# Two grouped-query attention blocks on one core: remainder scores in groups of three steps, remainder of P by DMA in some steps, output tiles kept in the accumulator

## The chip, the core and the metric

The kernel runs on one core of a Trainium2 chip. The metric is device time in microseconds (us) of one execution. Before the change the median of three runs is 721.26 us (721.23 to 722.15). The engines are named as in the profile: PE is TensorE (matrix multiply), PEld its weight loads, DVE is VectorE, ACT is ScalarE, POOL is GpSimd, and SP is SyncE, which here only issues DMAs.

## What is computed

There are two independent problems, A and B, of the same shape: 16 batches, 80 query rows each, model width 576, 32 query heads, 16 key/value heads, 512 cached keys, head width 128, all in bf16.

```python
q = (x @ wq).reshape(B, Sq, Hq, Dh).transpose(0, 2, 1, 3)
k = jnp.repeat(k_cache, rep, axis=1)          # rep = 2
v = jnp.repeat(v_cache, rep, axis=1)
scores = jnp.einsum("bhqd,bhkd->bhqk", q, k) * (Dh ** -0.5)
p = _softmax(scores, axis=-1)
o = jnp.einsum("bhqk,bhkd->bhqd", p, v)
out = o.transpose(0, 2, 1, 3).reshape(B, Sq, Hq * Dh) @ wo
# result: concatenate([out_A, out_B], axis=-1)
```

## The kernel before

**Steps.** The work is cut into 128 steps U, 64 for each problem. A step is one batch and four key/value heads, so 4 x 160 = 640 rows of scores (two query heads of 80 rows share one key/value head) against 512 keys. The 640 rows are taken as five tiles of 128: tiles 1 to 4 hold the first 128 of the 160 rows of each key/value head, and tile 0, the *remainder*, holds the last 32 rows of all four heads. 512 keys of one tile fill one PSUM bank; there are eight banks.

**What a step does on each engine.**
- SP loads K for two steps in one DMA transpose (1 MB, L626) and V for one step in a plain DMA (512 KB, L630).
- PE makes the scores. Tiles 1 to 4 are one full 128x128 matmul of 512 columns each (`qk`, L673). The remainder is four matmuls of 32 output rows side by side in the array (`qkr`, L660). The remainder scores of a *group* of steps are issued together; the sizes of the groups come from `GRP` (the first ones) and `GR` (all others), and a group takes one PSUM bank for each of its steps.
- DVE takes the row maximum (L682), ACT the exponential with its row sum (L686), DVE the reciprocal (L692), POOL the scaling (L695, `nrm`). The result is P in bf16, in `p_sb`: `NPA` slots for tiles 1 to 4 and `NPR` slots for remainders.
- PE transposes P (`tr`, L727): 40 small transposes in a step, 8 for each tile, each of a 64-row half. They go in pairs, one for each half of the array's rows. Each half has one PSUM bank for tiles 1 to 4 (`vtp`) and one for the remainder (`vtq`). DVE or ACT copies the first into `pT` (`ptev`, L738 or L740) and the second (`prev`, L745 or L747).
- PE multiplies by V (`pv`, L770, 4 x 4 matmuls of 160 columns), and DVE or ACT copies the result into `oT` (`oev`, L784).

**Beside the steps.** The projection of Q (`qp`, L537, four matmuls of 320 columns for one head and half a batch group; `qt`, L550, two 64-row matmuls that add the last 64 of the 576 input columns) is spread over the steps as 128 sessions. A session before step `US0` has its `qt` for itself (`pre`), a later one has it at the head of the transposes of a step, and shares the two banks `vtq` with the remainder's transposes. DVE or ACT then evicts Q (`qev`, L563 or L564). The output projection (`op`, L816, 2 x 8 matmuls of 288 columns for an output tile) runs twice for each problem over eight head pairs; the first pass lands in `acc` (L828), the second is added to it on DVE into one of two buffers `osb` (`oeb`, L845) and stored by SP (`st`, L851). x is loaded first, into the memory of `acc`, in pieces that `XLD` places.

**The order.** Nothing is decided at run time. Each operation is added to a list with the stream it belongs to, and the string `ORDER` says, letter by letter, which stream is next; an apostrophe takes the second engine of an operation that DVE or ACT may do, a digit gives the PSUM bank. That sets the order on every engine and the buffers' waits: an engine stops at an instruction until the semaphores for what it reads, and for the buffer it writes, have come. The constants `LA`, `GRP`, `TS0` and the like set keys within a stream.

Of the kernel before, what the change touches and what calls it, by code (L numbers as in the profile page):

```python
# [11 lines left out]
GRP = (1, 1, 2)  # L12
GR = 2
LA = 11.5
# [3 lines left out]
NPR = 4  # L18
NPT = 2
# [11 lines left out]
US0 = 2  # L31
# [16 lines left out]
XLD = ((-100.0, -60.0), (-5.0, -4.9))  # L48
# [11 lines left out]
LETTERS = "abcdefghijklmnopqrstuvwxyzABCDEFGHIJKLMNO"  # L60
ORDER = """
nEKni7KHHHHHHNj3Ej4IMk5j6MNIj7j3Mk4ILd6Id5IIdd2AaBd1dd5BAd6dd2'Bd1dd6BMd0AdAd7'BAd5Ldd4'A'Bd6dd5'ABKMd7add3'AB
d4e0doe1'Be2'Ad5ole7of6ld3ole0pe1dlod4omd2Ke7A'BhdCloe6vhf5Cald3oud0lBupf12luAdme7puo'BOmg0456Cpu'Ae1y'wOe3'xl
vj0oj4d5'zuCMj7loe6ud0moue1dMlk2Md4Llok7e2c3'AFBcle6hod5a'sLldog0137'BAe2'yCd5CCvw'zoj3e0lue7Mj4o'xve3lc6Mcuc1
locuof24ld0tu'spc7lucpg16muCtme3uzd2'youe7e6'wd4'xho'AFlg15oalBc3Cz'xe0u'wcle7Bc5uoc'yf46v'ACsle1oud2'tpd3ulc5
# [12 lines left out]
15z'w'ye2pb3'x'Bhomc7hCAculae0e1od4ubplComuc6e0qd2luog35slCuf17x'yBc'wu'zpe0d3'tomc5cCpc6u'Ae2le1scvod4'tvog05
lhuhle6zb2a'yCoume1we0vod5'x'Bc7Aulcoc4cld3t'se6e1log47ole0bCCo'wulzud6'x'yBe1u'Ae7Coc4ld3uo'qe5hvclag02sulof1
4u'wxlAc7cp'yb6p't'ze0e7moe2c5cBlbCouod3lvCc1slue0qcd5omuhhf27tlug46pe0y'wb1'zC'xou'Be6mFbvolue2qc4'Ae5olcac3s  # L80
d1CCpcud4'toulg06vb3'wzluA'xue2me6Bboyld4oe1Fc7od5lhqg02lf36'wz'Ae1xcCoc4u'sce2Blhud7od5'tp'ye1Ke4lob0mCoue2bl
puolvg13lc4z'ycc2q'se1acmoe0e4b3xlCCou'td6Bulwd2ovg15AluCf07w'zCve4'ype5b'AuomFoue1lKc6xd0uKo'qe4lhd3uolcuBc5c
'se2ltg16aob5p'w'zClxuc4ce6u'se2obmCB'Aud4olve0Cc7lod3u'ycug26ltrf17'ywChxve0'zpc5h'AcuDoe2'Be6'sc4oumck3ohuc5
lctd1'sLle0c4d5loe2coalg36C'tud0w'zyue4'xd6'Bolg35AlCpuc2c'yze1vc4'w'xoe3'Ab5umolBe0coc7'te6e1lscCe4oule2baoul
oe0ld3Coud6'sClrug17oluCf45z'yvc2p'wc'xd7uA'tmc1Bucpe2lc3vFoce6mDud4thloe0hg35soe2'zb1o'x'yCwe5luBbColue6lrud3
oDd4luhe0'Ag12holaCf57luyc6z'wvc'x'Ae0pc1'sue2'Bcome6c3pd4lCcCou'td5moug01lsue7z'wc3'xuclBd2ov'Ae1'yd5olg46Ctu
lhf07zhv'ye3pc1'wud4'Aomce2pc6lcod0'shC'xe3tu'Bc1aocle6ub5Cslvome1uc3ocg27u'te3'yzbloe2lrb7ole1e6loe5e3bDolaCC
xlb2uo'Buod6'wluCAd1lruc4g05uf37uy'zc'xwvd5Bpe0bhpmDAc1csd3C'thrumCg46JouDlf12xuwBc7'yczue0e4sc3cpb7'thoGc3ole
6bolCAe0luce5sb4urvoDe7d3ovle6boalome0d5Crlpg14lb7wx'ACov'zc3e6ucoe4'tbu'yomuBc3crhluc5CDe1d7luoclsd2hCvlg36DJ
u'tf04y'w'Aue1'ze5oe7ue3b6Caolupbluomd5xr'Bc1olcd6Cpluc2cvg07tsue2zme1b3Gw'xC'yoJue7oKd4luc0Blcoe2c6'Ascle1oe5  # L90
d0'tolg67oCe2z'xbulov'w'Be1re7'Aud0lCod3ulyKg45uClohuf26Jw'yxKCe1'zupc4hc'ABuc5mae0pcvlc3ocud2ts'sle7d3ome5Cg1
4ovlc6ulxcwod0u'Be7A'yd3o'te1lzg26lCouf45'w'zxd7Aulpe6hc0'yDcoc1'Bacsme2Cc3puclc0ok4umctd6vC'sLe1lug35'toue4'z
e0ob2lo'ye5we1lCbxuBloue6e4'Aoc3lacd7olc5ocld0sC'te1rulg36ovf25'yzue4lpe3b6wmxpc1'Acoh'Bd2mhCCc7svDe0lochud5o'
te1lug47oluCe3xblyuo'zue0e1'wBd4luaod5'Aole7g23rlof06'wz'yc1'xCcp'Auc3le2Bcuc4C'sod5mupe1clue0Coc7mcvhsd2Dot't
ve4lDg67uhlohd3ux'yhze1e0'Bd6o'wlc7oe2lcAc4c'sCoe5ulhg17tulof04v'zCxb2p'wulyd7u'BAmc5pe1cc3msce0ohe6'td5oalg34
olCe1ub'zo'yvxle0wd3CuB'Arc4lucoe2c7uod5le1'scolg06tlCf24zu'yDe7pe1uhb6xamwvCobuplud2Cmrc7uoe0'Ae6c'BuCoc3lcuo
d4lsug15lCtvf07'x'yve6p'wb3'zuBhobuDAlFe1c4moce2e6lod5d0olc1rclDg23t'shpe1'ye6Cwb4umAxuze2'BboCoc7lucc3lsvd5rc
uoe0Dd4thlg67oaf12w'zCCub3'xp'Avyme7e5uobloule1rc6ulcod3Be0lc7Cocud4'tslCg15vhDe7u'zxb6ao'wu'ACyle0e5bpomd3r'B
c7oe1lcoc4'se2d6lCovcg07u'tluf45w'xy'zd1uF'Bpe0luhd7Ac6moucpg23'slc4ze6cob0yle3FbmoaC'tCe2xule6oe5b4uolure3'wb
louolvd2CBe0'Aud6qloug57f14z'x'Bc3y'wc'Ae7d6'sDold3hCplue2c5Ccomug07hplvc1t'xucC'zwe2c5'yuod7'Bcu'se0lthe3uc1o  # L100
ac'Ac5'socme2d6tloe1b4Cloue0lvg35oluby'zxlwe1Ce2uo'Bf35'Aoue0ld6qvFld7phc4ocmc2se1lcpg34htae0y'zb2'xC'w'BuAc3m
# [165 lines left out]
def bass_concat_heads__gqa_block_cached__gqa_block_cached__near_ridge_kernel(  # L267
# [27 lines left out]
    with ExitStack() as es:  # L295
# [32 lines left out]
        def R(res, ver):  # L328
            return (res, ver)
# [281 lines left out]
        for U in range(NSU):  # L611
# [103 lines left out]
            def em_tr(e, psls=tuple(psls), vtq=vtq, vtp=vtp, td=td):  # L715
# [214 lines left out]
```

## Time and profile before

| | value |
|---|---|
| median of three runs | 721.26 us |
| the profiled execution | 722.56 us |
| its span, first to last instruction | 720.6 us |
| granted clock of TensorE | 1.000 |
| PE busy | 715.3 us, 99% of the span |
| DVE and ACT busy | 641.3 and 639.8 us, 89% each |
| POOL busy | 432.6 us, 60% |
| DMA moved | 160.73 MB |

The profile was taken in one execution. Busy time of PE is made of modelled ends: a matmul's record lasts longer than the time until the next one may start, because matmuls are pipelined, so what a matmul costs in a row of others is read from the starts. An engine's idle time is given with the instruction that released it. DMA issues are those of SP; "to landing" counts from the issue to the last byte.

### The profile page before, as it was taken

What the parts mean: (1) busy time and instruction counts of PE and PEld (TensorE: products, weight loads), DVE (VectorE), ACT (ScalarE), POOL (GpSimd) and SP (SyncE); (2) the same over time, 40 slices, a digit from 0 to 9 for tenths busy, and PEclk for the clock granted to TensorE, in tenths of its full rate; (3) what the DMA queues carried; (4) which work ended last, traced back from release to release, by engine and by line L of the source; (5) the groups of instructions that cost most, each with busy time, mean ns of one, the idle gap of its engine ahead of it and who ended that gap; (6) DMA issues with size and microseconds to landing.
All of it is one profiled execution on the core that took longest, in us unless ns stands there. A gap on an engine that the chain in (4) does not pass through costs nothing.

```text
span 720.6 us, 26290 instructions
## 1 busy us (share of the span) xinstructions
PE 715.3 (99%) x10820; PEld 513.1 (71%) x10820; DVE 641.3 (89%) x1459; ACT 639.8 (89%) x1844; POOL 432.6 (60%) x650
## 2 busy tenths in 40 slices
PE   9999999999999999999999999999999999999998
PEld 5567767777677777777777777777777777777777
DVE  3999998899888998899998899979999889998995
ACT  1999999799989998789997899989999889998993
POOL 0477755566556675665675567646676656755773
PEclk9999999999999999999999999999999999999999
DMA  9999999899999999999999998999999898988860
GB/s 248 268 269 259 265 255 241 206 189 259 225 241 209 217 254 240 226 254 205 268 207 219 248 245 212 247 236 204 181 262 224 193 241 198 220 194 200 178 199 18
DMA packets 374167, 160.73 MB, mean 223 GB/s; under 512 B 278560, under 2 KB 370976, under 8 KB 374048
## 3 DMA queue, kind: packets, MB, share of 16 engines
q1 hardware_dynamic: 374048, 159.05, 95.6%
q8 instruction: 86, 1.41, 0.8%
q14 instruction: 33, 0.27, 0.1%
HBM read 87.65 MB, written 2.95 MB: 126 GB/s over the span
## 4 chain that ended last, share of the span: by engine, by line
PE 98%; ACT 1%; issue 0%; DVE 0%
PE ps L816 22%; PE ps L770 20%; PE ps L537 19%; PE ps L673 16%; PE ps L727 11%; PE ps L660 5%; PE ps L550 4%; ACT p_sb L686 1%; PE ps L348 0%; PE ps L396 0%; ACT qT L563 0%; PE ps L414 0%; PE ps L451 0%; DVE osb L845 0%; DVE wo_sb L341 0%
## 5 line engine op out<-in xcount | busy, mean ns | idle before, releaser
L695 POOL TENSOR_SCALAR p_sb<-p_sb,rinv 128x512 bf16<-128x512 bf16 x640 | 430.8, 694 | 272.7 <-DVE rinv L692 272.2
L686 ACT ACTIVATE p_sb<-ps,negmax 128x512 bf16<-128x512 f32 x640 | 444.0, 711 | 29.8 <-DVE negmax L682 25.5
L682 DVE TENSOR_REDUCE negmax<-ps 128x1 f32<-128x512 f32 x640 | 419.2, 681 | 27.5 <-PE ps L673 22.2
L770 PE MATMUL ps<-pT,v_sb 128*128 128x160 bf16 x2048 | 191.1, 233 | 0.1
L770 PEld LDWEIGHTS ps<-pT,v_sb 128*128 128x128 bf16 x2048 | 154.0, 98 | 39.5 <-ACT pT L745 3.3
L816 PE MATMUL ps<-wo_sb,oT 128*128 128x288 bf16 x1280 | 181.6, 286 | 0.0
L673 PE MATMUL ps<-kT,qT 128*128 128x512 bf16 x512 | 176.4, 381 | 0.0
L537 PE MATMUL ps<-xT,wq_sb 128*128 128x320 bf16 x1024 | 176.0, 299 | 0.0
L816 PEld LDWEIGHTS ps<-wo_sb,oT 128*128 128x128 bf16 x1280 | 122.1, 98 | 43.2 <-ACT p_sb L686 1.7
L686 ACT ACTIVATION_READ_ACCUMULATOR p_sb<-ps,negmax 128x1 f32 x640 | 144.0, 225 | 0.0
L537 PEld LDWEIGHTS ps<-xT,wq_sb 128*128 128x128 bf16 x1024 | 94.5, 98 | 42.4 <-ACT p_sb L686 2.2
L727 PEld LDWEIGHTS ps<-ident,p_sb 64*128 64x128 bf16 x5120 | 91.4, 95 | 8.8 <-issue 1.1
L727 PE MATMUL ps<-ident,p_sb 64*128 64x64 bf16 x5120 | 96.1, 190 | 1.2 <-ACT qT L563 0.7
L738 ACT COPY pT<-ps 128x512 f32<-128x512 f32 x150 | 88.4, 603 | 9.4 <-PE ps L727 9.0
L740 DVE COPY pT<-ps 128x1024 bf16<-128x1024 bf16 x106 | 72.0, 684 | 13.2 <-PE ps L727 11.7
L563 ACT ACTIVATE qT<-ps 128x320 bf16<-128x320 f32 x131 | 59.5, 462 | 16.2 <-PE ps L550 15.4
L784 DVE CAST oT<-ps 128x320 bf16<-128x320 f32 x129 | 61.5, 482 | 6.5 <-PE ps L770 6.0
L564 DVE TENSOR_SCALAR qT<-ps 128x320 bf16<-128x320 f32 x125 | 59.5, 482 | 8.1 <-PE ps L550 6.6
L673 PEld LDWEIGHTS ps<-kT,qT 128*128 128x128 bf16 x512 | 48.4, 97 | 25.7 <-issue 3.3
L784 ACT CAST oT<-ps 128x320 bf16<-128x320 f32 x127 | 56.4, 448 | 10.2 <-PE ps L770 9.9
L745 ACT COPY pT<-ps 128x128 f32<-128x128 f32 x132 | 36.1, 288 | 7.0 <-PE ps L727 6.8
L692 DVE RECIPROCAL rinv<-rowsum 128x3 f32<-128x3 f32 (+1 forms) x256 | 39.5, 161 | 2.3 <-ACT p_sb L686 2.2
(31 smaller groups left out, 194.7 us busy)
## 6 DMA issues: line engine op xcount, KB each, us to landing
v_sb<-in_A_v_cache_dram SPq DMA_DIRECT2D x64, 512.0 KB, 5.4
v_sb<-in_B_v_cache_dram SPq DMA_DIRECT2D x64, 512.0 KB, 4.9
wo_sb<-in_A_wo_dram SPq DMA_DIRECT2D x8, 576.0 KB, 5.6
wo_sb<-in_B_wo_dram SPq DMA_DIRECT2D x8, 576.0 KB, 5.6
wq_sb<-in_B_wq_dram SPq DMA_DIRECT2D x4, 1024.0 KB, 6.6
out_dram<-osb SPq DMA_DIRECT2D x40, 72.0 KB, 3.4
wq_sb<-in_A_wq_dram SPq DMA_DIRECT2D x8, 256.0 KB, 4.5
wq_sb<-in_A_wq_dram SPq DMA_DIRECT2D x2, 1024.0 KB, 7.3
```

The source lines that it names most:

```text
L537: last = e.matmul(ps[:, vbq[h].phys, QO:QO + 320], lhsT=wq_sb[:, wsl, ck, hi * 128:(hi + 1) * 128], rhs=xT[:, half, ck, n0:n0 + 320], star ...
L563: return e.activation(dst, src, AF.Identity, scale=SCALE)
L673: return e.matmul(ps[:, vb.phys, :], lhsT=qT[:, qsl, bl, gl * 160:gl * 160 + 128], rhs=k_of(U, gl), start=True, stop=True)
L682: return e.tensor_reduce(negmax[:, si:si + 1], ps[:, vb.phys, :], axis=AX.X, op=AluOpType.max, negate=True)
L686: return e.activation(p_sb[:, psl, :], ps[:, vb.phys, :], AF.Exp, bias=negmax[:, si:si + 1], scale=1.0, accum_out=rowsum[:, ss, k:k + 1])
L695: return e.tensor_scalar(p_sb[:, psl, :], p_sb[:, psl, :], rinv[:, ss, k:k + 1], 1.0, op0=AluOpType.mult, op1=AluOpType.mult)
L727: last = e.matmul(dst, lhsT=p_sb[64 * h:64 * h + 64, psls[k_], j * 128:(j + 1) * 128], rhs=ident[64 * h:64 * h + 64, 64 * h:64 * h + 64], ...
L738: return e.copy(pT[:, pts, :, :].bitcast(F32)[:, :, 32 * h:32 * h + 32], ps[:, vtp[h].phys, :].rearrange("p (n c) -> p n c", n=16))
L740: return e.tensor_copy(pT[:, pts, :, 64 * h:64 * h + 64], psb[:, vtp[h].phys, :].rearrange("p (n c) -> p n c", n=16))
L770: last = e.matmul(ps[:, vo.phys, off:off + 160], lhsT=v_sb[:, vs, gl, j * 128:(j + 1) * 128], rhs=pT[:, pts, 4 * gl + j, :], start=(j == 0 ...
L784: return (e.copy if en == "act" else e.tensor_copy)(dst, src)
L816: last = e.matmul(ps[:, vb.phys, 0:DC], lhsT=oT[:, sp_ * (HH // 2) + i, rb * 128:(rb + 1) * 128], rhs=wo_sb[:, 2 * c3 + sp_, i, :], start= ...
```

## The change

- `GRP` and `GR`: after two groups of one and three groups of two, the remainder scores are issued for three steps at a time instead of two.
- In the odd steps from 71 to 123 (`RT0`, `RT1`, `RTM`, `RT2`) the remainder of P is not transposed by PE: SP issues one DMA transpose from `p_sb` into `pT` (128x512 bf16), which waits for POOL's scaling and for the readers of the old `pT`. PE then does 32 instead of 40 transposes, and the two copies of the remainder fall away; `pv` also waits for the DMA.
- `pT` is laid out by block of 128 keys, tile and row instead of by head, block and row, so that the DMA's target is one run for each block. The transposes of tiles 1 to 4 now write two runs of 32 columns instead of one of 64, those of the remainder one run of 64 instead of two of 32; the copies write longer runs; `pv` reads its 160 columns as five runs of 32.
- The final output tile is written (in bf16) over its own tile of `acc`, and stored from there; `osb` is gone.
- `NPR` goes from 4 to 5, `US0` from 2 to 0, `LA` from 11.5 to 11.0, and the second half of the first part of x is placed later among the first loads.
- `ORDER` is another string. It moves instructions on every engine through the whole program, and deals the copies to DVE and ACT anew.

```diff
-GRP = (1, 1, 2)
-GR = 2
-LA = 11.5
+GRP = (1, 1, 2, 2, 2)
+GR = 3
+LA = 11.0
...
-NPR = 4
+NPR = 5
...
-US0 = 2
+US0 = 0
+RT0 = 71
+RT1 = 124
+RTM = (0, 1)
+RT2 = 999
...
-XLD = ((-100.0, -60.0), (-5.0, -4.9))
+XLD = ((-100.0, -85.0), (-5.0, -4.9))
...
-        pT = sb("pT", [128, NPT, 16, 160], BF16)
+        pT = sb("pT", [128, NPT, 4, 5, 128], BF16)
...
-        osb = sb("osb", [128, NOSB, DC], BF16)
...
+            rtr = RT0 <= U < RT1 and (RTM[U % 2] or U >= RT2)
-            vtq = td["vb"] if td else [S.bank() for _ in range(2)]
+            vtq = td["vb"] if td else [] if rtr else [S.bank() for _ in range(2)]
...
-                for n_ in range(20):
+                for n_ in range(4 if rtr else 0, 20):
                     k_, j = divmod(n_, 4)
                     for h in range(2):
                         if k_:
-                            c_ = ((k_ - 1) * 4 + j) * 64
-                            dst = psb[:, vtp[h].phys, c_:c_ + 64]
+                            dst = psb[:, vtp[h].phys, 256 * j:256 * j + 256].rearrange("p (i n) -> p i n", i=2)
+                            dst = dst[:, :, 32 * (k_ - 1):32 * k_]
                         else:
-                            dst = psb[:, vtq[h].phys, 0:256].rearrange("p (g j c) -> p g j c", g=2, j=4)[:, :, j, :]
+                            dst = psb[:, vtq[h].phys, 64 * j:64 * j + 64]
...
+            if rtr:
+                def em_rtr(e, psl=psls[0], pts=pts):
+                    return e.dma_start_transpose(pT[:, pts, :, 4, :], p_sb[:, psl, :])
+
+                S.add("sp", 5.0 * U - 0.4, em_rtr, reads=[R(("P", psls[0]), ("n", 5 * U))],
+                      writes=[R(("pR", pts, h), U) for h in range(2)], dsem="d_r%d" % pts, name="rtr%d" % U, stream="RT")
...
-                S.add(en, ts + 0.45 + 0.1 * h, em_prev, reads=[R(vtq[h], 0)],
-                      writes=[R(("pR", pts, h), U), R(("tb", pts, h), U)], name="prev%d.%d" % (U, h), stream="prev%d" % h, alt=EV)
+                if not rtr:
+                    S.add(en, ts + 0.45 + 0.1 * h, em_prev, reads=[R(vtq[h], 0)],
+                          writes=[R(("pR", pts, h), U), R(("tb", pts, h), U)], name="prev%d.%d" % (U, h), stream="prev%d" % h, alt=EV)
...
-                                        rhs=pT[:, pts, 4 * gl + j, :], start=(j == 0), stop=(j == 3))
+                                        rhs=pT[:, pts, j, :, 32 * gl:32 * gl + 32], start=(j == 0), stop=(j == 3))
...
-                                return e.tensor_tensor(osb[:, slot, :], ps[:, vb.phys, 0:DC],
+                                return e.tensor_tensor(xs[:, rb, 2 * c3 * DC:(2 * c3 + 1) * DC], ps[:, vb.phys, 0:DC],
                                                        acc[:, rb, c3 * DC:(c3 + 1) * DC], AluOpType.add)
...
-                                return e.dma_start(dst, osb[:, slot, :])
+                                return e.dma_start(dst, xs[:, rb, 2 * c3 * DC:(2 * c3 + 1) * DC])
```

More of the change, by code (lines that the diff above doesn't have):

```diff
@@ L58 @@
 WOK = 6.0
-LETTERS = "abcdefghijklmnopqrstuvwxyzABCDEFGHIJKLMNO"
+LETTERS = "abcdefghijklmnopqrstuvwxyzABCDEFGHIJKLMNOPQ"
 ORDER = """
[L62 to L65, printed above, removed]
@@ L126 @@
[L126 to L128 removed]
+pGMpk7JJMJJJPKl3Gl4JOl5m6OKNKOPl3Kd4Kd5Kead6DCd7d4d5d2d1eee'CDd0CD'Dd6Cd4l5ed7CDd2Od6Oem3Dd5MNd7CMeae'Dd3'Dg0'
+Cg1'Cqh7h2qg6nd4qnd5rend0rog1Ceqg6'Dd3'Cqog7d4Dng5qjl2d0njEOwaeqng1d6xEq'Dg2'Cwh47Eqnwerd3nwrg5od1QDwoECi46qxn
@@ new lines @@
+l7Awg0'y'zl2nOg4wOg7'Bqm5wg2'Dd6N'Cqnc1g5qcnd3jqang0l4q'uOni17qnEh24ywznCc5Qrg6'Awcq'Dg0l1x'Bd3Evnwc7rcod5wuc6
+oOg7qm2Hi14EEnNxjcy'BwHd2q'vjwg0'Azg6jEqg4nwc1acDnwud7qwg1i05qnwq'zng6Eywq'Bc4Awng5cDxg0'Cc1q'Ccnd3qnh27EuwEd6
+nrwg1'vrd5owqi04oxg2A'yw'zc7ncEqg0x'vg1Dnd7wqg6wBb2nEq'Cwag4i03bA'znB'Dc0cyEc7qx'uc'Cc3qg0'swcnvc5wcqnd7wvg1nj
+d6qj'ui45Eawy'Bwzh023Ang5r'Dd4'Crd6ori17oqog0d2B'Aqc3ncc7Eyxg1znCg5cqw'Dc4'ug0Ecwqnc3cuw'vjg6qg1nd4jwqa'vg7ni3
+5qnb0zE'ABw'Dg6qng5xbqnwqd3'ynECg1wc7sng4cqwh026'uEqnwd5Ernwi17rowrc4'yxjc'Ad0B'Cwg1'zvg3od7Daqoi45qnc2zcA'Bg6
@@ new lines @@
+c1'DEd5qnwg7ug4'yxcnqg2b3E'vqnqg1ng6bEqxHnCjwg7nqc4HcwEg0sj'uc2qcnwjd3aqnwi14vnwEh267A'Bx'yg0r'zd4w'Crd1owDb5o
+wrwg2qoi36qng7Bb'Aq'zng0yc3Dncqg2c6'ucs'Cc7Eqng1wcc3qnwcg0g5'uqd4Eqv'vnd7wi23nwEEng1Bwjg0b6'ya'Azwq'Dg2xqg5nc7
+qcwnc3d1qwncCd0nEuwi24'vwh357'Azx'y'Bg2rb'Dqog0rc4jncqjd3'soug2b6qng5'Cd4qani01nbA'B'yEr'Cwg0g1zc3oqxg2cc5E'sw
+qcnc7qwd6nDcwd0'vunvg1g5qji34jEqnxg2Lb7B'Aw'zqng1wd3yqng4c5qabnEC'Dwd2Enswcc7'ucwi46wh015'A'Bb4r'v'zE'y'Dwg7Cc
+6ord2wIg3qjcxbjunLEqwoc6jg0Escwnd7rwg1qoi34x'vb5wy'z'AC'Bqg2g6ng4Dd3qng0c7qnacc1Eqcnwg2bqnxuwnd6EsEwi47qwg0A'z
@@ new lines @@
+b5'Dwq'Bw'yd4nCc7Eg6nwcqg2'ubxEqnxjd3vnwIi67'swh012A'Bw'y'zg5rc7'DcCd3ord4qoi06Er'vwg1'ABb7wnqg0oyg6qbanCqg2nc
+3g1qcng0qd5'snc6ucqg7'vd3znqi26nEDwc1EnBd4xLzc'y'Ag0jwc7'uqLg6'Dg2wcjq'Cd3nwqc5cnEg0vwc1'uqacnxi67vnEwh125B'Aw
+zg0'yrg7w'Cc6'Dcqc4ob3r'uqod6Ernwcg1vd2nwqi04ojg7jnybEqw'AB'zg1xg0'Dqd5'swng2ECg4wd3qnawi67qnEc1w'Azcyqc0'Bxc'
+uDg6c7nwqg1d3nqcd2nEvwg4E'Cc0qwcni56ujw'vjnh017wBj'Ayxg4r'zb6'Cqog5g3nqbErnwc4cs'Dwg0qog5c6ad2r'uncqd4ovi13qnE
+g7zwnb6Eqw'DBg0'Ag5xEd4nqwd3qnbxyj'Cjwni17jwg0'zg2w'BDc5c'sqc7'Acyng6qjc3g1q'uc'vg0c5qnad7Cncd2vnui46qh135'BEA
@@ new lines @@
+x'y'zb6E'Crwnrwc7og4Dcwqc0og2g1wucnEd3qw'vd7rnwi04Eqxjg2ynjbwA'Bwqg0'zg1qb4nDoqc2g7ncsc5Ccng0Eujd3x'vqad6wqni2
+5wg1y'zg7'Bqb'AEqnc5d2E'CxE'sDg0cnwqc3cnug6wd4vnwqi15wnh037jBw'y'Ag6b5w'Cqrng1Hd2zr'DboEqwc4r'sg0xg6ocqad5wnEu
+b3wnqwoi14g0A'zg7'BbqnD'yg1g4q'Cc6ncqg2d5'vjqnc0Hcsnc6qcd3nji17'ug0A'Bb4nEEzwqg1d7wEqnd2wEbv'DM'yxCg0w'sc3qcnc
+4wEcuni56xEwvh013yBw'Cjb4'AzMwrbwrHoarxg7og6Dd5woqc2wg0qcnc3wqcnd1sg7'uvi46nqEg2'Awg0qb3nwqng4xg7qbnq'Bd2ynzd6
+Etjw'CEg0Mni34qw'Dwc5'ABg1cnwqc7g4'ycu'zg0'Cqjc3ncaEg2qd5wnDd1w'uvni46qEh037wA'Bnxc6rc'yd4'zwCoc2rc'Dd5r'uog0v
@@ new lines @@
+i12qog6Eyj'Ac3wqg7'Bcaxd1znqc2w'Dcvc0nCcEg5u'vwd3qng0wm4qng2i67qnNb5'B'znEg0g7wqb'Aw'DEqH'yg2nwd3jqnFg6xd4Ctnx
+i01qEh257'AzB'Dc0'yrng1caEc4Cx'ucroc6cwvc3'ug0qwcog2qd4wng6qd5wnvb1wqnrng0i23EqowFg6EB'zbxj'Ajqnwg2Dd3'ywnqg0g
+7wEd5tnqFwi16'Cqjnwac4ycBng2c0q'Acg7'ug6Cd1'znqc3qg4ncd2DnEui57x'vEqwh036'BA'zw'yc7ED'Ccwrg5nd2qw'vd1orjwi47nj
+rwc0'ABcg5'zEog4Dwd7q'yc1'uwcqnc3jxd0vncg1'Cc5qag4'uci23nvqg5b1Bnq'yg3'Abqnzog2ECd4wqng7wg6tc5ncEEDwd3Fqb2xjEq
+nwg0g1'uqbxnaqwni57twnh026Bw'z'DEg1yw'Ab7rwqog5wbrCxoc3qg0nd4qcntg2jd1ErnwIc7cqL'vwc5Fi03nFc'Bzd2uoEvg3wb7q'y'
@@ new lines @@
+DwAng1g6qb'CEqnwg0c3tang5wqd4xg1qni67b0'AzEqwng6Bcw'ynbCxq'uc7Eng1wcc3jvcwc6qF'ug2d5'DLEqwcd3t'vwnFi47xjjh016'
+ABnzd4r'Dg7rd2ob3qMor'yg0nbqoi17tnEwc3y'Bg0cwqC'Cc7g6d4nMucFg5q'Ag3Mb0'zq'Da'vEqg1nxg2c7qnwbnwcg6nud5qi37tqc1n
+b0zB'DnIcEEwg2jg7'yqd5'CLw'vd6Eqa'AwbnExni34wtwh012y'zB'Dw'Cg7rg6'Ad4wqoc3wcrc5nd0xr'ucqoi37voEc1Bwg5ncqg2wc7'
+z'Acud6'yDng1qg0'Cc3Lqcnc4jvd5'uFEqng2wji37EqnjwFcz'Bwg1yjm0D'Ad7Cwanqg5g6xc3'vqcnc4qc'ub2nN'vg1g5nEEqwh034qwn
+bErwnd6rwoi15rwotd0wozAg2d3x'Bq'yg1x'DCi45nqg7'Azg6Bc2'Dg4a'ycEqnwc3cqd5nwqc1'Cc'uvg7d0nuc3qncg1Eg2nwqi46'vwqn
@@ L129 @@
+vx'uEqnwg1tc7ncqwi2456'uEwg0'Ayg7xqc2FncjbEwqnfv'Bg1tg0ni25Ezjxqh346F'Aqwnc7rwg2'Bcb1qnwuowc5rcwg0vc7ocqg5nc3E
+cqwbnfvwnui0234tFi57'Azayg1E'Brg0wb3qowEg2qnwbqnwc4g1nxcqb6'BtnEc7uwg0'Acqjwi1234'vFg7F'yg5nqbj'BFqnc1Ectwg0'z
+c4Fnqcwh267unEvwi15'Arg0x'Bg4qc3ob5wfErnwcqog2wjbqnjxAc6'uctni0134vFErg5jw'Bg2c6yocqwc4cq'uxg0nb7qnvg6Eg5'Azbw
+qnqwc3ncEtwc4ncFi1267w'u'vg0y'Ag5Eqb1w'Bq'zwnc7g2xncqc3c'ug0E'vi4567wqnwbznBx'yb5'AEwc7wcc3i0246bA'z'Byucc4vcc
+7tctb6F'vuFbb7tFbtF
 """
@@ L322, in bass_concat_heads__gqa_block_cached__gqa_block_cached__near_ridge_kernel @@
                      + ["d_out%d" % i for i in range(NOSB)]
+                     + ["d_r%d" % i for i in range(NPT)]
                      + ["d_k%d" % i for i in range(NK)] + ["d_v%d" % i for i in range(NV)])
@@ L730, in em_tr @@
                 return last
-            S.add("pe", ts, em_tr, reads=[R(("P", psls[k_]), ("n", 5 * U + k_)) for k_ in range(5)] + [IDENT]
+            if rtr:
[3 more added lines that the diff above has]
+                      writes=[R(("pR", pts, h), U) for h in range(2)], dsem="d_r%d" % pts, name="rtr%d" % U, stream="RT")
+            S.add("pe", ts, em_tr, reads=[R(("P", psls[k_]), ("n", 5 * U + k_)) for k_ in range(1 if rtr else 0, 5)] + [IDENT]
                 + (td["reads"] if td else []),
@@ L844, in em_eb, with em_st @@
                             def em_eb(e, rb=rb, c3=c3, vb=vb, slot=slot):
-                                return e.tensor_tensor(osb[:, slot, :], ps[:, vb.phys, 0:DC],
+                                return e.tensor_tensor(xs[:, rb, 2 * c3 * DC:(2 * c3 + 1) * DC], ps[:, vb.phys, 0:DC],
                                                        acc[:, rb, c3 * DC:(c3 + 1) * DC], AluOpType.add)
-                            def em_st(e, rb=rb, c3=c3, prob=prob, slot=slot):
+                            def em_st(e, rb=rb, c3=c3, prob=prob):
                                 dst = out.rearrange("b s d -> (b s) d")[rb * 128:(rb + 1) * 128,
                                                                         prob * D + c3 * DC:prob * D + (c3 + 1) * DC]
-                                return e.dma_start(dst, osb[:, slot, :])
+                                return e.dma_start(dst, xs[:, rb, 2 * c3 * DC:(2 * c3 + 1) * DC])
                             S.add("dve", xe, em_eb, reads=[R(vb, 0), R(("acc", rb, c3), (prob, hh - 1))],
-                                  writes=[R(("osb", slot), (prob, half, n))], name="oeb%d.%d.%d" % (prob, half, n),
+                                  writes=[R(("acc", rb, c3), (prob, hh))], name="oeb%d.%d.%d" % (prob, half, n),
                                   stream="oeb")
-                            S.add("sp", xe + 0.3, em_st, reads=[R(("osb", slot), (prob, half, n))],
+                            S.add("sp", xe + 0.3, em_st, reads=[R(("acc", rb, c3), (prob, hh))],
                                   dsem="d_out%d" % slot, name="st%d.%d.%d" % (prob, half, n), stream="st")
```

113 lines of the change are left out of this document (39 added, 74 removed).

## The prediction, made before the changed kernel ran

> **What bounds the kernel now.** First the page's busy times and the chain that ended last:
>
> ```profile
> PE 715.3 (99%) x10820; PEld 513.1 (71%) x10820; DVE 641.3 (89%) x1459; ACT 639.8 (89%) x1844; POOL 432.6 (60%) x650
> ...
> PE 98%; ACT 1%; issue 0%; DVE 0%
> ```
>
> PE has no idle time to speak of, and the chain is PE's own instructions one behind the other. So the time is the sum of what PE issues, plus the little it waits. What one instruction costs there is not its mean duration but the distance to the next start. PE's timeline gives that, here from 400.88 us (start, duration, engine, line, count):
>
> ```profile
> 400.88 0.31 PE L550 MATMUL ps<-xT,wt 64*128 64x320 bf16 x2
> 401.03 0.75 PE L727 MATMUL ps<-ident,p_sb 64*128 64x64 bf16 x40
> 401.70 0.61 PE L660 MATMUL ps<-kT,qT 128*32 128x512 bf16 x8
> 402.25 0.72 PE L537 MATMUL ps<-xT,wq_sb 128*128 128x320 bf16 x4
> 402.81 0.38 PE L673 MATMUL ps<-kT,qT 128*128 128x512 bf16 x1
> 403.02 0.71 PE L537 MATMUL ps<-xT,wq_sb 128*128 128x320 bf16 x4
> 403.56 0.72 PE L770 MATMUL ps<-pT,v_sb 128*128 128x160 bf16 x8
> 404.21 0.31 PE L550 MATMUL ps<-xT,wt 64*128 64x320 bf16 x2
> ```
>
> The 40 transposes hold PE for 0.68 us, the remainder scores of two steps (L660, x8) for 0.55. I took the starts of all 10,820 matmuls in this way. They repeat to a nanosecond: 8 transposes 116 ns, two 3 ns apart and the next pair 26 later; L660 548 ns for two steps, 331 for one; eight L770 553 ns before other full-array work. In the last two rows they take 650 (403.56 to 404.21): what follows there (L550) uses half the array, and that change costs 96 ns. A single score matmul shows the same, 216 ns before full-array work and 312 before L550, L660 or L727. With a median for each kind, PE's instructions add up to 711.8 us; waits are 4.9, and 3.9 lie before and behind (span 720.6).
>
> ACT decides one place, the fill. The chain from 18 to 36 us:
>
> ```profile
> 20.01 0.77 ACT qT L563 x2
> 20.77 3.35 ACT p_sb L686 x10
> 24.12 0.33 ACT qT L563
> 24.45 3.35 ACT p_sb L686 x10
> 27.79 0.34 ACT qT L563
> 28.13 0.04 issue
> 28.18 0.76 PE ps L727 x40
> ```
>
> Ten records are five exponentials, 0.67 us each, without a break; the first transposes wait for them. Then the DMA issues (KB each, us from issue to landing), and one stretch of the table of windows:
>
> ```profile
> v_sb<-in_B_v_cache_dram SPq DMA_DIRECT2D x64, 512.0 KB, 4.9
> ...
> kT<-in_B_k_cache_dram SPq DMA_TRANSPOSE x32, 8.4
> ```
>
> ```profile
> 560.00:690.00 130.00, 130.00 (x2001) 94.36 (x1998) 116.97 (x263) 118.91 (x346) 81.86 (x123) 1.00 0.89 206
> ```
>
> V lands 4.9 us after its issue, K (1 MB, two steps) 8.4, in the order of issue. In the stretch PE is busy for all 130.00 us, and beside it the DMA share is 0.89 at 206 GB/s. Room is there, little of it.
>
> **The change part by part, on PE.** The counts come from the built orders of both kernels.
> - *Transposes*: 27 odd steps from 71 to 123, 8 fewer each: 27 x 116 ns = 3.13 us off.
> - *Remainder scores*: now 63 x 548 + 2 x 331 = 35.19 us; then 2 x 331 + 3 x 548 + 40 groups of three. A further step costs 217 (548 - 331) to 225 ns (first to fifth start within an L660 row); I take 220, so 768 a group and 33.02 in all: 2.17 off.
> - *Changes of array shape*: entries from full-array work into L550, L660, L727 (or x's transposes) fall from 150 to 144, 6 x 96 ns = 0.58 off. An L550 pair that full-array work follows pays 242 ns instead of 146; there are 13 now, 9 then: 0.38 off.
> - *Strided access*: `pv` reads five runs of 32. No row shows a split read. From below nothing; from above one column lost at each of the four joins, 4 x 0.42 ns (213 ns for 512 columns) x 2048 = 3.5 us. The nearest row is a split write: the first eight transposes of a step write two runs of 32 today and take 116 ns, the next 24 write whole runs of 64 and take 350, the same for eight. I take 0 for both. [...]
>
> Together 3.13 + 2.17 + 0.58 + 0.38 = 6.26 us off PE.
>
> **Beside PE.** The 54 copies of remainders that fall away (288 ns on ACT, 282 on DVE) take some 15 us from two engines at 89%. They lie under PE, and save nothing of themselves; without PE's cover they would show only in the fill, where none is removed. The output tile in `acc` is the same DVE operation (449 ns), and SP's store waits for it as before; the buffer was not waited for at the end, where tiles come 1.96 us apart and a store lands in 3.4 with two buffers. So 0. `NPR` 5 gives remainders a slot more, which three banks at a time and the DMA's late read need: 0.
>
> **New waits: the fill.** Up to a given place in its order PE has some work since the first score, and needs some exponentials and copies from ACT, which starts about 1.4 us later (first score, maximum). Before, at the transposes of step 1: PE 14.50; ACT 17 exponentials (0.677 back to back), 4 Q evictions (0.341), 4 copies, 13.99 + 1.4: PE is 0.9 late. After: PE 14.89; ACT 17 exponentials, 6 Q evictions, 4 copies, 14.67 + 1.4: 1.2 late. At the third `pv` of step 2: 24.63 against 28 exponentials and the rest, 24.84 + 1.4: 1.6. At the transposes of step 5: 32.84 against 33.39 + 1.4: 2.0; before, 34.20 against 33.99 + 1.4: 1.2. So ACT alone gives 0.8 more. DVE is as tight, and the moved piece of x lands behind the first piece of wq and its remainder, up to 1.2 us later, with five transposes and `xev` waiting. Ends 0 and +4; I take +2.0.
>
> **New waits: the DMA.** SP now waits for POOL's `nrm` in 27 places; behind it stand a V load in 17 cases, K in 6. In the new order PE has between 3.1 and 14.5 us of work from the DMA's place to `pv`. If it landed like V, 4.9 us, eight of the 27 fall short, by 5.9 us in all; like the fastest V loads (3.8), one by 0.7. It has a quarter of V's bytes. Its issue holds SP between 0.5 us (an eighth of the fastest K, 3.95) and 2.2 (a straight line through x's 640 KB, 3.18, and K's 1 MB); I take 1. K that comes later meets groups of three, which need it a step sooner. I take +0.8, ends 0 and +6.
>
> **Sum.** -6.26 + 2.0 + 0.8 = -3.5 us. Against the profiled span 720.6 that is 717.1, and its execution 719.1 of 722.56. Against the median, 1.3 below that execution: **717.8 us**.
>
> **Rivals.**
> 1. *The work goes and waits take its place.* With fill +3.5 and DMA +2, 720.5 us: no change that shows. For it: PE waits 4.9 us in all today, so any loosening counts. Against: most steps have slack, 8.4 us in the median from `nrm` to `pv` in these odd steps today.
> 2. *Slower: SP's issue.* The transpose out of SBUF holds SP like a K load, 3.95 us, and lands 3 later, 7.9. Then 20 of the 27 places are short, by 46 us in all; a wait also gives the next ones slack, so about half: 721.3 - 3.5 + 23 = 741. It decides from about 2.2 us of issue. For it: no row shows a transpose from SBUF, and SP's K issues last 4 to 9.5 us. Against: those move eight times as much. [...]
> 3. *Split reads cost.* With 3.5 us on `pv` there is nothing left: 721.3.
>
> **Chances.** Forecast 0.64, rival 1 0.15, rival 2 0.16, rival 3 0.05. 0.2%, 1.44 us, is about what can be told from no change. Faster by more: the forecast, 0.64. Same: rival 1 with part of 3 and the forecast's upper edge, 0.16. Slower: rival 2 and some of 1 and 3, 0.20. Range: below, 721.3 - 6.3 with no new wait is 715.0; above, the forecast with fill and DMA at their upper ends, 721.3 - 6.3 + 4 + 6 = 725. Rival 2 stays outside, 0.16.
>
> **What would show it.** Right: 4,904 matmuls at L727's place; groups of three take 765 to 775 ns to the next start, 32 transposes 116 ns less than 40, eight `pv` 553 ns still; PE's idle time mostly before 80 us, behind ACT; the new DMA's issue near 1 us, its landing under 5. Wrong: L770 waiting for a DMA again and again between 410 and 700 us, K's scores waiting for `kT`, SP issues of several us at the new line, `pv` spacing above 69 ns, or a fill that ends more than 4 us late.

## The result, and the profile after

The changed kernel takes 726.57 us (median of 4 runs, 724.92 to 727.10) against 721.25 before: a ratio of 1.0066, 95% interval 1.0054 to 1.0078. It is slower by 0.66%, where 717.8 us was forecast. The profiled execution took 724.92, the fastest of the four; its span is 723.1 us (before: 720.6).

The page of after, busy times and the chain that ended last:

```profile
PE 710.3 (98%) x10604; PEld 510.5 (71%) x10604; DVE 631.2 (87%) x1417; ACT 637.2 (88%) x1832; POOL 432.2 (60%) x650
...
PE 89%; DVE 4%; ACT 3%; DMA 2%; SPq 1%; issue 0%
```

PE is busy 5.0 us less and ends later. The chain, 98% PE before, is 89% PE and goes through DVE, ACT and the DMAs as well. The table of windows tells where; first before, then after (PE, PEld, DVE, ACT, POOL busy, granted clock, DMA share, GB/s):

```profile
0.00:80.00 80.00, 78.10 (x1030) 50.33 (x1031) 66.40 (x155) 63.78 (x187) 40.90 (x69) 1.00 1.12 264
400.00:560.00 160.00, 160.00 (x2481) 115.36 (x2480) 144.74 (x327) 148.96 (x432) 99.91 (x149) 1.00 0.99 228
```

```profile
0.00:80.00 80.00, 74.95 (x966) 46.77 (x967) 63.95 (x150) 59.51 (x173) 38.85 (x65) 1.00 1.06 241
400.00:560.00 160.00, 156.73 (x2356) 112.48 (x2354) 143.21 (x313) 144.29 (x416) 98.90 (x148) 1.00 1.03 228
560.00:690.00 130.00, 128.62 (x1910) 94.15 (x1909) 117.31 (x259) 115.47 (x328) 81.29 (x121) 1.00 1.02 219
```

PE loses time in the fill and in the stretch with the DMA transposes. There the DMA share has gone from 0.99 and 0.89 to 1.03 and 1.02: by this measure the room that the prediction saw beside 206 GB/s is gone. The share adds up the packets' times over 16 engines and is not bounded by 1 (in the fill of before it is 1.12, at 264 GB/s), so "full" means no more below than a share near 1 in this stretch.

For a ledger I took, at points along PE's order, the start of an instruction less the cost of all that stand ahead of it (the medians of the prediction); the difference is what PE has waited so far.

| profiled execution, us | before | after | change |
|---|---|---|---|
| PE's instructions | 711.4 | 705.0 | -6.4 |
| waited up to 80 us | 3.56 | 7.65 | +4.1 |
| 80 to 400 us | 1.98 | 1.68 | -0.3 |
| 400 to 690 us | 0.76 | 5.86 | +5.1 |
| the rest, to PE's end | 0.28 | 0.34 | +0.1 |
| PE's end | 718.0 | 720.5 | +2.6 |

The other three runs of the changed kernel are 1.3 to 2.2 us longer than this one, and the profiled execution of before is 1.3 us above its median. So the profiled executions are 2.4 us apart (724.92 and 722.56) and the medians 5.3; no profile shows where the other 3 us lie.

One of the three largest stops of the stretch, in the timeline (SP, then PE; start, duration; in brackets the idle time before and its releaser):

```profile
484.29 8.52 SPq L630 DMA_TRANSPOSE kT<-in_B_k_cache_dram  x1
492.85 1.47 SPq L634 DMA_DIRECT2D v_sb<-in_B_v_cache_dram  x1
494.36 0.62 SPq L510 DMA_DIRECT2D wt<-in_B_wq_dram  x1
495.10 1.23 SPq L739 DMA_TRANSPOSE pT<-p_sb  x1
```

```profile
498.28 0.44 PE L780 MATMUL ps<-pT,v_sb 128*128 128x160 bf16 x4
500.43 0.45 PE L780 MATMUL ps<-pT,v_sb 128*128 128x160 bf16 x4 [1.71 <-DMA pT<-p_sb]
```

P's remainder of step 85 was scaled at 488.2 and the old reader of `pT` done at 488.8. SP came to it at 495.1, because it had sat in the issue of a K load for 8.5 us and two more DMAs stood behind that. It landed at 500.38; PE started `pv` at 500.43. The other two large stops, 1.1 us at 431 and 1.5 at 681 (steps 73 and 119), end on landings too, at 432.39 and 682.38, but SP was hardly late there: it issued at once and 1.0 us after the inputs were ready, and the transfers took 6.8 and 5.7 us to land. (The profile puts these two stops down to ACT and DVE; PE started 0.09 us after each landing.) All 27, the issue in ns and the landing in us:

```profile
L739 SPq DMA_TRANSPOSE pT<-p_sb x27: 1188/1191/2222, 415.5 to 697.0; - x27
...
DMA to landing us min/median/max: 2.4/4.2/6.8
```

Nine of them land later than the 4.9 us that V took before.

SP's own queue, what the new line waited for (total us, times, longest):

```profile
SPq L739 <- PE ps L677: 17.2, 6, 5.5
SPq L739 <- PE ps L826: 11.4, 3, 5.8
SPq L739 <- PE ps L780: 8.7, 5, 2.6
SPq L739 <- POOL p_sb L699: 8.6, 8, 2.7
SPq L739 <- PE ps L541: 5.1, 2, 2.9
SPq L739 <- PE ps L732: 3.8, 3, 1.5
```

8.6 us are waits for POOL's scaling, the only ones that the prediction counted. The other 46 are for PE. `pT` has two slots, all 27 steps are odd and so use the same one, and the transfer must wait until `pv` of two steps earlier has read it. In 18 of the 27 steps that came later than the scaling, and in 14 of them SP issued 30 to 32 ns after the end of that `pv` (the lines named are those of the instructions around it). Whatever stands behind it on SP, K and V, waits too.

In the fill the chain has gone over from ACT to DVE (pieces in order of time: start, duration, what):

```profile
20.06 3.08 DVE negmax L686 x5
23.14 0.40 DVE qT L568
23.54 1.20 DVE negmax L686 x2
24.74 0.40 DVE qT L568
25.14 0.60 DVE negmax L686
25.82 0.31 DVE xT L405
```

So it goes on to 37 us, and again from 42 to 45: maxima, evictions and copies of DVE almost without a break, where the chain of before had ACT's exponentials up to 28 us and PE from there.

### The profile page after: what moved, and what is told of

Its sections match the earlier page's. It is cut to its first block, busy times and chain, and to the rows that moved or that the text cites. A ratio compares the mean times of both kernels' runs of the same rounds, so it can differ in the third digit from the quotient of the medians.

```text
span 723.1 us, 25846 instructions
## 1 busy us (share of the span) xinstructions
PE 710.3 (98%) x10604; PEld 510.5 (71%) x10604; DVE 631.2 (87%) x1417; ACT 637.2 (88%) x1832; POOL 432.2 (60%) x650
## 3 DMA queue, kind: packets, MB, share of 16 engines
q1 hardware_dynamic: 388736, 162.59, 99.2%
## 4 chain that ended last, share of the span: by engine, by line
PE 89%; DVE 4%; ACT 3%; DMA 2%; SPq 1%; issue 0%
PE ps L826 21%; PE ps L780 19%; PE ps L541 17%; PE ps L677 15%; PE ps L732 9%; PE ps L664 4%; PE ps L554 4%; DVE negmax L686 3%; ACT p_sb L690 2%; DMA v_sb<-in_A_v_cache_dram 1%; DMA wq_sb<-in_A_wq_dram 1%; DMA pT<-p_sb 1%; DVE qT L568 0%; ACT qT L567 0%; SPq L506 0%
## 5 line engine op out<-in xcount | busy, mean ns | idle before, releaser
L690 ACT ACTIVATION_READ_ACCUMULATOR p_sb<-ps,negmax 128x1 f32 x640 | 142.0, 222 | 0.0
L751 DVE COPY pT<-ps 128x1024 bf16<-128x1024 bf16 x114 | 77.6, 685 | 21.0 <-PE ps L732 20.3
L750 ACT COPY pT<-ps 128x512 f32<-128x512 f32 x142 | 83.5, 596 | 12.4 <-PE ps L732 11.9
L732 PEld LDWEIGHTS ps<-ident,p_sb 64*128 64x128 bf16 x4904 | 88.2, 95 | 6.4 <-DVE rinv L696 0.4
L732 PE MATMUL ps<-ident,p_sb 64*128 64x64 bf16 x4904 | 92.3, 190 | 0.0
L567 ACT ACTIVATE qT<-ps 128x320 bf16<-128x320 f32 x149 | 65.6, 455 | 20.2 <-PE ps L554 16.2
L568 DVE TENSOR_SCALAR qT<-ps 128x320 bf16<-128x320 f32 x107 | 51.0, 481 | 9.9 <-PE ps L554 7.1
L554 PE MATMUL ps<-xT,wt 64*128 64x320 bf16 x256 | 39.2, 306 | 1.0 <-ACT oT L794 0.5
```

Of the source, the lines that this page charges most:

```text
L554: last = e.matmul(ps[:, vbq[h].phys, QO:QO + 320], lhsT=wt[64 * h:64 * h + 64, wsl, hp, :], rhs=xT[64 * h:64 * h + 64, half, 4, n0:n0 + 32 ...
L690: return e.activation(p_sb[:, psl, :], ps[:, vb.phys, :], AF.Exp, bias=negmax[:, si:si + 1], scale=1.0, accum_out=rowsum[:, ss, k:k + 1])
L732: last = e.matmul(dst, lhsT=p_sb[64 * h:64 * h + 64, psls[k_], j * 128:(j + 1) * 128], rhs=ident[64 * h:64 * h + 64, 64 * h:64 * h + 64], ...
L750: return e.copy(dst.bitcast(F32), ps[:, vtp[h].phys, :].rearrange("p (j n) -> p j n", j=4))
L751: return e.tensor_copy(dst, psb[:, vtp[h].phys, :].rearrange("p (j n) -> p j n", j=4))
```

## The experiments

All times are medians; the kernel before, run beside them, takes 721.4 to 721.7 us. 726.57 is the changed kernel.

### The layout alone

Before's order and constants with the new layout of `pT` and the output tiles in `acc`, no DMA transposes.

```diff
-GRP = (1, 1, 2, 2, 2)
-GR = 3
+GRP = (1, 1, 2)
+GR = 2
...
-RT0 = 71
+RT0 = 999
```

> The old order and constants (groups of two, no DMA transposes, US0 2, NPR 4) with the new layout of pT and the output tiles in acc: the order on every engine is that of the kernel before. Theory 'split reads cost nothing': 721.3 within 0.7. Theory 'split reads or writes cost': 723 or more, with eight pv taking over 553 ns or eight transposes over 116.

721.20 us, ratio 0.9995 (0.9986 to 1.0003). Split writes, split reads and the tiles in `acc` cost nothing that shows in this kernel.

### The remainder's transfer, taken apart

Five kernels keep the changed kernel's order and take something from the transfer. In the first four the 27 steps use an older remainder, in the fifth the remainder as it stands, not transposed. First, no transfer at all:

```diff
-            if rtr:
-                def em_rtr(e, psl=psls[0], pts=pts):
-                    return e.dma_start_transpose(pT[:, pts, :, 4, :], p_sb[:, psl, :])
...
```

> As x2_scratch, but with no DMA transposes at all: the remainder of P is left out in the 27 odd steps (neither PE nor DMA transposes it). This is the changed kernel with PE's saving and without any price of the DMA. Theory 'late at pv': as x2, 722 or below. Theory 'queue': 4 us or more below x2. Theory 'fill': as the changed kernel, less than 1 us below it. If fill and PE work were as forecast, 721.3 - 6.3 + 2 to 4 = 717 to 719.

Second, the transfer lands in a scratch tile, so `pv` doesn't wait for it; SP still waits for `pv` of two steps earlier:

```diff
-                    return e.dma_start_transpose(pT[:, pts, :, 4, :], p_sb[:, psl, :])
+                    return e.dma_start_transpose(xst[:].rearrange("p (j a) d -> p j (a d)", j=4), p_sb[:, psl, :])
```

> The changed kernel, but the DMA transposes write into a tile that nobody reads (the old xst, made 256 B longer), and pv of the 27 odd steps reads what step 69 left in pT; each DMA still waits for nrm and for pv two steps earlier. So the remainder of P is wrong in those steps; PE, SP and the DMA engines do the same work. Theory 'late at pv': PE stops because the transposed remainder has not landed; without that wait the three stops of the profile (1.9 + 1.5 + 1.1 us) go and the median falls from 726.6 to 722 or below, and the differences from run to run with it. Theory 'queue': the DMA and its waits in SP's order delay K and V; the time stays at 726 and the stops move to L677, L664 and V. Theory 'fill': the loss is before 80 us, the time stays at 726.

Third, the second kernel without SP's wait:

```diff
-reads=[R(("P", psls[0]), ("n", 5 * U)), R(("pvd", U - 2), 0)],
+reads=[R(("P", psls[0]), ("n", 5 * U))],
```

> As the run with the scratch target (723.09: the 27 DMA transposes land in a scratch that nothing reads, pv uses an older remainder), but SP no longer waits for pv two steps earlier, only for P's normalisation. Theory A (SP's waits for TensorE, 46 us in the profile of after, delay the loads behind them): 721.3 to 722.3, and SP's waits for PE at this line gone. Theory B (the transfers' share of the queue costs, not SP's waits): 722.8 to 723.5.

Fourth, all the waits, but next to no transfer:

```diff
-                    return e.dma_start_transpose(pT[:, pts, :, 4, :], p_sb[:, psl, :])
+                    return e.dma_start(tok[0:16, pts, :], p_sb[0:16, psl, 0:32])
```

> The changed kernel, but the 27 DMA transposes of 128x512 are plain copies of 16 x 64 bytes at the same places of SP's order, with the same waits of SP (for P's normalisation and for pv two steps earlier) and the same wait of pv for the transfer; the remainder that pv uses is an older one. Theory A (what costs is the order: SP stands waiting for pv two steps earlier, loads queue behind it, and pv then waits for a transfer that stands behind others): 724.5 to 726.5. Theory B (what costs is the transfer's own service, about 0.6 us of the queue each and its 1.19 us of issue): 721 to 723.

Fifth, the same 128 KB, not transposed:

```diff
-                    return e.dma_start_transpose(pT[:, pts, :, 4, :], p_sb[:, psl, :])
+                    return e.dma_start(pT[:, pts, :, 4, :], p_sb[:, psl, :].rearrange("p (j n) -> p j n", j=4))
```

> The changed kernel, but each of the 27 DMAs copies the remainder's 128x512 block (the same 128 KB, in pieces of 256 bytes) without transposing it, with the same waits of SP and of pv; the remainder that pv uses is so not the transposed one. Theory A (the transposing is what is dear: in the profiles 27 transposes take 33 us more of the queue's sixteen engines than the same kernel without them, 1.2 us each, where 128 KB at the profile's mean of 223 GB/s are 0.6): 722 to 724, and a queue share of about 95 to 96%. Theory B (any transfer of 128 KB at these places costs this much): 725.5 to 727, and a share of 98 to 99%.

| transfer | SP waits for `pv` | `pv` waits for it | us | ratio (95%) |
|---|---|---|---|---|
| none | no | no | 720.98 | 0.9990 (0.9981 to 0.9999) |
| 16 x 64 bytes | yes | yes | 721.05 | 0.9986 (0.9975 to 0.9998) |
| 128 KB transposed | no | no | 721.25 | 1.0000 (0.9987 to 1.0014) |
| 128 KB transposed | yes | no | 723.09 | 1.0026 (1.0012 to 1.0040) |
| 128 KB copied | yes | yes | 722.23 | 1.0008 (0.9999 to 1.0017) |
| 128 KB transposed | yes | yes | 726.57 | 1.0066 (1.0054 to 1.0078) |

Against no transfer, neither the waits alone (+0.1 us) nor the volume alone (+0.3) costs anything that can be told from no change. Together they do: volume and SP's wait 2.1, and `pv`'s wait for the landing 3.5 more. (The kernel before, run beside the rows, took 721.25 to 721.68; by the ratios these four steps are -0.3, 0.7, 2.6 and 2.9 us.)

The first two kernels fit their theories only in part. Without a transfer it is 720.98: below 722, as 'late at pv' had it, but 2.1 below the scratch kernel and not level with it (nor 4 below), and above the 717 to 719 that PE's work and the fill as forecast would give. PE's 6.4 us less and the fill's 4.1 more would give 719.2, so 1.8 us remain unexplained. The scratch kernel should have fallen to 722 or below, or stayed at 726, and is at 723.09. In its profiled execution (721.68) PE's largest stop of the stretch is 1.6 us at the remainder scores (L664, 516.01 us), on a K load that landed at 515.92: with `pv` set free, part of the loss moves to K.

Of the two expectations for the small copy the one that held put the cost on the transfer's service; with SP's wait taken away the one that held put it on that wait. Both theories were half of one: SP's wait costs 1.8 us (721.25 to 723.09) with 128 KB to move, and both waits together 0.1 (720.98 to 721.05) with 1 KB. The windows of the small copy, of the scratch without SP's wait and of the scratch with it:

```profile
400.00:560.00 160.00, 159.84 (x2387) 115.07 (x2386) 146.13 (x318) 147.19 (x424) 99.64 (x149) 1.00 0.93 222
```

```profile
400.00:560.00 160.00, 159.22 (x2382) 114.75 (x2381) 145.36 (x317) 146.75 (x423) 99.75 (x149) 1.00 1.05 232
```

```profile
400.00:560.00 160.00, 157.79 (x2366) 113.73 (x2364) 144.35 (x316) 145.47 (x418) 99.51 (x148) 1.00 1.05 231
```

With a DMA share of 0.93 all of SP's waits leave PE 159.84 of 160 us of work; with 1.05 and no wait for `pv` it has 159.22; with 1.05 and SP's wait 157.79; in the changed kernel, with 1.03 and both waits, 156.73.

What one transfer takes of the queue follows from the packets' share of the span, with none and with the scratch without SP's wait:

```profile
q1 hardware_dynamic: 374048, 159.05, 93.4%
```

```profile
q1 hardware_dynamic: 388736, 162.59, 97.9%
```

That is 97.9% of 720.2 less 93.4% of 719.3 us, 33.3 us or 1.23 us for each of the 27, where 128 KB at the mean of 223 GB/s are 0.6. It is 544 more packets for each. The plain copy has 528, and 97.3% of 720.5, 1.08 us: my expectation of a share of 95 to 96% was wrong, and the transposing is not what makes the pieces dear for the queue. The copy holds SP for less (0.62 against 1.19 us) and lands sooner (3.8 against 4.2 us in the median), and the kernel is 4.3 us faster with it; whether the one or the other does it was not told apart.

### How many

> The changed kernel with the DMA transpose only in every fourth step (71, 75 to 123: 14 of the 27); the other 13 odd steps use the remainder of two steps earlier and have no transfer of their own. Theory A (the loss grows from the point where the queue has no room left: before's share of 0.89 to 0.99 leaves room for some of them): under half of the 5.6 us that the 27 cost, 721.5 to 723. Theory B (each transpose costs its own 0.2 us, wherever it stands): 723.5 to 724.

721.74 us, ratio 1.0005 (0.9994 to 1.0015). Against no transfer 14 transposes cost 0.8 us, 27 cost 5.6. So it is not a fixed price for each. That the loss sets in where the queue is full is not shown by this run: with 14 transposes the share from 400 to 560 us is 1.02 (after: 1.03), and PE is busy for 159.36 of the 160 us in the profiled execution, the fastest of the twelve. That there are half as many waits can be the reason as well.

### The transposes in before's order

The 27 transposes added to the order of before, in groups of two. Their places in SP's queue were my choice, each behind the scaling and behind the `pv` of two steps earlier as they stand in the order, so the time is no measure of the change.

> The kernel before (groups of two, its fill and its order) with the new layout and the 27 DMA transposes; in SP's order each stands behind nrm and pv of two steps earlier, as early as the old order allows. PE does 216 transposes less, 3.1 us. Theory 'late at pv': SP's place is not better than in the changed kernel, PE stops several times behind pT; 721 to 727. Theory 'fill': without the new fill it keeps the saving, 718 to 719. Theory 'queue': slower than 721 with stops at K and V rather than at pv.

733.44 us, ratio 1.0164 (1.0149 to 1.0180). The groups, the fill and the queue's room are those of before, PE has 216 transposes less to do, and it is 12 us slower; none of the three expectations is met. The two largest stops are at `pv`, not at K or V. SP and PE at the largest:

```profile
468.30 9.43 SPq L630 DMA_TRANSPOSE kT<-in_B_k_cache_dram  x1
477.77 1.26 SPq L739 DMA_TRANSPOSE pT<-p_sb  x1
```

```profile
480.39 0.83 PE L780 MATMUL ps<-pT,v_sb 128*128 128x160 bf16 x5 [5.68 <-issue]
```

The remainder stands right behind a K load whose issue holds SP for 9.4 us. It is what happened to step 85 in after, at a worse place.

### The fill

> The changed kernel with the order of before for its first 342 operations (to about 50 us), and the order of after behind it. In the profiled run of after, TensorE had lost 7.65 us by 80 us against 3.56 in before. Theory A (the fill's 4.1 us are lost for good, because TensorE sets the end): 726.6 - 2 to - 4, that is 722.5 to 724.5, and a loss of about 4 to 5.5 us at 80 us. Theory B (the stretch with DMA transposes is bound by the DMA queue, so a faster fill only makes TensorE wait longer there): 725.5 to 727, with the loss at 690 us again near 15.

> As the run before, and the remainder of P is neither transposed nor fetched in steps 71, 73 to 123 (those steps use an older remainder). Theory A (fill and DMA are the two things that ate the 6.4 us that TensorE's instructions save): 717.0 to 718.5, against 720.98 without the remainder but with the new fill. Theory B (the groups of three themselves cost slack on the K loads and the banks): 719.5 to 721.

Both set `US0 = 2` again and take before's order for the first 342 operations. 725.26 us (ratio 1.0046, 1.0029 to 1.0063), and without the remainder 718.87 (0.9950, 0.9938 to 0.9962), both between the bands of the two theories. The ledger at 80 us falls from 7.65 to 4.67, for 1.0 us more of PE's instructions: 2.0 net. Without the remainder that comes through (720.98 to 718.87). With it 1.3 do, less than the two intervals can tell apart, for the loss from 400 to 690 us stays (5.60 waited by 400 us, 11.81 by 690). Without the remainder PE has 5.4 us less to do than before (711.4 to 706.0), and 2.8 of them show; 1.1 of the rest is the fill's (4.67 against 3.56), and 1.5 stay open.

### SP's order

The last two move only DMAs in SP's queue, and all of the computation is done: in the first behind before's fill, in the second behind the changed kernel's own. In the second 169 of the 315 DMAs stand at another place of SP's queue; every other engine keeps its order.

> All of the computation, all 27 DMA transposes. The fill has the order of before (as in the first run of this kind, 725.26), and SP's DMAs stand at other places of SP's order, nothing else is moved: a replay in which the queue serves a transpose in 1.23 us chose the places so that K and V loads go out ahead of the waits. Theory A (the loss is the order of SP under a full queue, and can be had back by placing): 720 to 721.5, with the largest stop of TensorE behind 400 us under 1 us. Theory B (the transfers' volume costs whatever the order): 724 to 725.5.

> The changed kernel with its own fill and its own order on every engine; only SP's DMAs behind the fill are issued in the order of the 718.41 us kernel (169 of 315 stand at another place of SP's queue). Theory A (of the 8.2 us between the changed kernel and that one, SP's order gives nearly all, the fill 1.3 to 2): 720 to 721, every remainder transpose landed at least 1 us before pv could start. Theory B (the fill and the order only help together, because the early loss shifts every later load): 722.5 or more.

718.41 us (ratio 0.9957, 0.9944 to 0.9969), better than either theory said, and 720.49 (0.9986, 0.9977 to 0.9995). So of the 8.2 us between the changed kernel and the better one 6.1 are SP's order, and 2.1 the fill (with the fill first, through the kernel of 725.26, it is 1.3 for the fill and 6.9 for the order). The first is faster than both kernels, with all 27 transposes in it. Its windows, and its line for the transposes:

```profile
400.00:560.00 160.00, 159.70 (x2405) 114.95 (x2404) 146.15 (x318) 146.71 (x423) 99.48 (x148) 1.00 1.01 234
560.00:690.00 130.00, 130.00 (x1981) 95.15 (x1974) 118.00 (x263) 117.67 (x334) 84.76 (x126) 1.00 0.99 220
```

```profile
L739 SPq DMA_TRANSPOSE pT<-p_sb x27: 1190/1197/2211, 413.5 to 690.1; - x27
...
DMA to landing us min/median/max: 2.4/3.5/5.5
```

The queue is as full as in after (q1 99.5% against 99.2%), and SP still waits some 49 us at this line, 37 of them for PE (after: 55 and 46). What differs is what stands where. From the landing of each transposed remainder to the moment when PE has done all that stands ahead of its `pv`, the profiled execution of after had 2.7 us in the median, under 1 us in five steps and less than nothing in three (-1.8 at worst). This kernel has at least 1.5 everywhere; its transposes land in 3.5 us in the median and 5.5 at most, where after has 4.2 and 6.8. V pays: its loads had 16.3 us in the median and 6.4 at least, and now have 2.3 at least, with a median of 17 still. Loads with much time stood ahead of a transfer with none. In the second kernel one step is still short by 1.5 us and two more have under 1 us in the profiled execution, which was its slowest, so the expectation of at least 1 us everywhere was not met there.

## Why the prediction was wrong

**What held.** The instructions: 4,904 matmuls at L732, groups of three 764 ns (768 forecast), 32 transposes 116 ns less than 40, four `pv` matmuls 277 ns still: -6.4 us for -6.26. Nothing for the strided access, as the layout kernel shows (721.20 us, ratio 0.9995). The bound of 3.5 us on it holds with 0.42 ns a column as 216 ns for 512 columns, the distance from one score matmul to the next in the profile before; no row shows the 213 ns given for it. Nothing for the tiles in `acc`, by the same kernel; the copies that fall away and `NPR` were not tested by themselves. The issue: 1.19 us in the median and 2.22 at most for 1 forecast, so rival 2, which decided from 2.2, didn't happen, though the time ended on its side.

**The fill, +2.0, measured +4.1.** The forecast summed ACT's exponentials place by place, got 0.8 us from them and put the rest on DVE and x without a sum ("DVE is as tight"). In the profile the fill's chain runs mostly through DVE: DVE is 4% of the whole chain where before has 0. PE waits 3.3 us between 30 and 60 us where it waited 0.5, 0.7 more up to 30 (with 1.3 us for the moved piece of x) and 0.6 more behind 60. The range given was 0 to +4, and its middle was taken without a sum for the engine that became the bound. Before's order of the fill takes the wait from 7.65 to 4.67.

**The DMA, +0.8, measured +5.1 in the profiled execution, and 5.6 between the medians without and with the transfers (720.98 and 726.57).** This is the step that failed. "SP now waits for POOL's `nrm` in 27 places" counted one of the two waits. That the transfer also waits for the old reader of `pT` was in the change's own description, and 46 of SP's 55 us of waits there are for that. The order of SP's queue was not priced either: with the same transfers, the same kinds of wait and every other engine's order kept, another order of SP is 6.1 us faster. The 3.1 to 14.5 us of PE's work "from the DMA's place to `pv`" take SP to be at that place when PE is; at step 85 it came 6.3 us late. "If it landed like V, 4.9 us, eight of the 27 fall short, by 5.9 us in all" was nearer to what came, and I set it aside because "it has a quarter of V's bytes". It lands in 4.2 us in the median, but in 4.9 or more nine times and 6.8 at most, and takes 1.2 us of the queue: with a share of 0.89 from 560 to 690 us before, 14 us were free in that stretch by that measure, and the twelve transposes in it need 14.8. The prediction quoted that row and did not divide it. Dividing would have said that the room is gone, not that PE must wait: the kernel of 718.41 us has the same twelve there at a share of 0.99, and PE is busy for all 130.00 us.

**The sum.** -6.4 + 4.1 - 0.3 + 5.1 + 0.1 = 2.6 us in place of -3.5, for the profiled executions. Between the medians it is 5.3, and for the difference there is no account. Rival 1, where waits take the place of the work, was the right kind, with 5.5 us of new waits where 9.2 came; it stopped at no change because it gave the DMA +2.

## What to carry to other kernels

A transfer that is moved to a DMA queue is priced three times: its time in the queue (1.23 us here) against the room that the stretch has left, its issue on the engine that issues (1.19 us), and the order there, where it waits for its inputs and for the last reader of its target (55 us for the 27) with every load behind it. Here, with a share of 0.93, the waits cost nothing that showed (721.05 us against 720.98), and with a share near 1 the order decided between 726.57 and 720.49 us for the same transfers. So order by slack: what has 16 us to spare goes behind what has two.

## What was not expected of the hardware

- That SP's K issues last 4 to 9.5 us stood in the prediction; that a 128 KB transfer that stands behind one goes out up to 6.3 us after its inputs are ready (after, step 85), did not.
- The 128x512 bf16 transfer from SBUF to SBUF made 544 packets and took 1.23 us of the queue when transposed, 528 and 1.08 when copied in pieces of 256 bytes: about twice the 0.6 us that its 128 KB are worth at the mean of 223 GB/s.
- The time of one kernel spreads: 722.48 to 727.28 us in seven runs with before's fill, where before, run beside it, stays within 720.36 to 722.88. A full queue is not shown to be the reason: the kernel with the small copies, at a share of 0.93, spreads from 718.55 to 723.32 beside the same.
